# Batch 0's second half: keys mixed two rows at a time, queries turned by full transposes, and a warm-up of 64 short and 5 wide matmuls

## The chip, the cores and the metric

The kernel runs on one core of one Trainium2 chip, in one launch. The metric is the device time of one execution in microseconds. A core has TensorE (matmuls and the loads of their weights, listed in the profile as PE and PEld), VectorE (DVE), ScalarE (ACT), GpSimd (POOL) and SyncE (SP). Each engine works off its own instructions in order and waits for others by semaphores; transfers go through DMA queues that SP and POOL feed here. Matmuls write to PSUM, and VectorE or ScalarE must copy a result out before its PSUM buffer can be used again.

## What is computed

Two layers follow each other. The first is a block-sorted attention: a small 8x8 matrix per head is normalized five times over rows and columns (Sinkhorn) and then mixes the eight blocks of keys and of values; each block of 96 queries attends only to its own mixed block. The second is a mixture of four experts over the attention's output.

```python
def _attn_ref(q, k, v, sort_net):            # q, k, v: (4, 8, 768, 64); sort_net: (4, 8, 8, 8)
    P = sort_net
    for _ in range(5):
        P = P - np.max(P, axis=-1, keepdims=True)
        P = np.exp(P)
        P = P / (np.sum(P, axis=-1, keepdims=True) + 1e-09)
        P = P / (np.sum(P, axis=-2, keepdims=True) + 1e-09)
    k_sorted = np.einsum('bhij,bhjcd->bhicd', P, k_b)      # k_b: k in 8 blocks of 96 rows
    v_sorted = np.einsum('bhij,bhjcd->bhicd', P, v_b)
    scores = scale * np.matmul(q_b, k_sb.transpose(0, 1, 2, 4, 3))
    attn = softmax(scores)
    return np.matmul(attn, v_sb)

def _moe_ref(x, domain_probs, w1, w2):       # x: (3072, 512); w1: (4, 512, 1024); w2: (4, 1024, 512)
    p = domain_probs / (domain_probs.sum(-1, keepdims=True) + 1e-09)
    for e in range(E):
        h = np.maximum(x @ w1[e], 0.0)
        out += p[:, e:e + 1] * (h @ w2[e])
```

## The kernel before

The order of the instructions on every engine is the order in which the kernel's text issues them; nothing reorders them. The work is staged by batch. Batches 1 to 3 go by plans of small steps slotted between the experts' matmuls. Batch 0 has its own code, because everything waits for it at the start; the change lies there, in the first 33 us.

Start: one DVE memset makes a constant tile `dummy`, and `warm(84)` issues 84 matmuls of 128x128 on it (L260) whose results nobody reads, while ScalarE and VectorE go through the five normalizations (L295 to L315). Within the fifth, the queries of the first half are transposed (`h_q`, L272) and 30 more such matmuls follow. When the normalized weights are there, they are spread by four matmuls (L327) and multiplied with a mask into `PI0`, a 128x64 matrix per head and half: a product with it mixes the blocks.

Batch 0's data lie in "natural" layout: partition p holds six consecutive rows (R = 6) of each head, so that sixteen partitions (CP = 16) are one block. The eight heads form two quads (`qd` 0, 1), the eight output blocks two halves (`hf` 0, 1) of four (HB = 4). `mix_half` makes one quad's half: for each head and each row r it multiplies a 128x64 slice of the keys (or values) as weights with the 64 columns of `PI0` (L506), 24 matmuls. Two heads write to partitions 0 to 63 and 64 to 127 of the same PSUM buffer, each on one half of TensorE's columns. `mixed` copies the buffer out (L517) with one copy of 128x768 when it takes a whole half. `h_k` does both for the keys, into `kTs[qd]`, the operand of the scores; `h_v` for the values, into `vT0[qd]`. `h_w` (L533) transposes mixed values back, `h_s` (L561) computes scores and their exponentials (L567), `h_a` (L578) multiplies with the values and normalizes (L591, L592), `h_x` (L609) transposes the result into `xTs[0]`, the input of the experts, and copies it out (L613).

Between these, the first layer of expert 0 runs in groups: `group0(qq, nq, g, kcs)` (L690) accumulates over the four chunks `kcs` of the 512 inputs and, after the last, ScalarE applies relu and writes `Hb` (L703). `second_layer0` (L725) multiplies with the second weights; after its first four matmuls of each output tile, and after each tile, it calls the next entry of the list `later`. The first entry is `h_q_both(1, vec)` and `h_w(1, vec)`: the 48 transposes of 64x64 for the queries of the second half, both quads, with two VectorE copies (L285), and a transpose of values.

Queries of batch 0 are loaded to `q0` (in the room of `Tt[3]`) by POOL's DMAs of line L147: quad 0 on partitions 0 to 63, quad 1 on 64 to 127. The second half's are issued at 12.6 and 13.3 us.

PSUM buffers come from two pools of two: `psm` (TensorE's results of the experts, and others) and `psa` (the attention's). A pool gives out a buffer again only when the last reader of what stood there is through; the matmul that writes to it first waits for that.

Of the kernel before, what the change touches and what calls it, by code (L numbers as in the profile page):

```python
# [9 lines left out]
F32 = mybir.dt.float32  # L10
F16 = mybir.dt.float16
# [6 lines left out]
def kernel(  # L18
# [11 lines left out]
    nc = tc.nc  # L30

    B, H, S, D = q.shape
# [6 lines left out]
    P = 128  # L39
    SCALE = float(D) ** -0.5  # L40

    CP = P // NB
    R = BLK // CP
# [3 lines left out]
    HB = NB // 2  # L47
# [75 lines left out]
    def head(b, nm, h):  # L123
        return natural[(b, nm, h // 4)][:, h % 4, :, :]
# [26 lines left out]
    dummy = Hflat[:, ds(2 * NFC * 2 * P, P)]  # L151
# [16 lines left out]
    ident = const.tile([P, P], F16, name="ident")  # L168
# [84 lines left out]
    qTs = {}  # L253
    q_ring = const.tile([P, 3, R, P], F16, name="q_ring")

    def warm(n):
        ps = psM.tile([P, 4, P], F32, tag="ps", name=f"ps_w_{state['n']}")
        state["n"] += 1
        for m in range(n):
            nc.tensor.matmul(ps[:, m % 4, :], dummy, dummy, start=True, stop=True)  # L260

    qT0 = [from_spare(2 * S).rearrange("p (s f r x) -> p s f r x", s=2, f=2, r=R) for _ in range(2)]

    def h_q(qd, hf, copy, ps=None):

        if ps is None:
            ps = psa([P, 2, R, 64], F16, f"ps_q_{qd}_{hf}")
        rows = ds(64 * qd, 64)
        for sg in range(2):
            for r in range(R):  # L270
                for hh in range(2):
                    nc.tensor.transpose(  # L272
                        ps[ds(D * hh, D), sg, r, :], q0[rows, hf, 2 * sg + hh, r, :], ident[rows, rows]
                    )
        if copy:
            copy(qT0[qd][:, :, hf], ps[:])

    def h_q_both(hf, copy):

        ps = psa([P, 2, 1024], F16, f"ps_q_{hf}")  # L280
        pss = [ps[:, qd, 0:2 * R * 64].rearrange("p (s r x) -> p s r x", s=2, r=R) for qd in range(2)]
        for qd in range(2):
            h_q(qd, hf, None, pss[qd])
        for qd in range(2):
            copy(qT0[qd][:, :, hf], pss[qd])  # L285
# [210 lines left out]
    def mix_half(nm, qd, hf, pool, warm_up=0):  # L496

        ps = pool([P, 1024], F32, f"ps_m{nm}_{qd}_{hf}")
        keep_warm(ps[:, 0:P], warm_up)
        tails[(nm, qd, hf)] = ps[:, 2 * R * 64:1024].bitcast(F16).rearrange("p (n x) -> p n x", n=2)  # L500
        ps = ps[:, 0:2 * R * 64].rearrange("p (s r x) -> p s r x", s=2, r=R)
        for sg in range(2):
            for r in range(R):
                for hh in range(2):
                    h = 4 * qd + 2 * sg + hh
                    nc.tensor.matmul(  # L506
                        ps[ds(D * hh, D), sg, r, :],
                        head(0, nm, h)[:, r, :],
                        PI0[hf][:, h, :, :].rearrange("p i c -> p (i c)"),
                        start=True, stop=True,  # L510
                    )
        return ps

    def mixed(nm, qd, ps, i0, n, copy):

        dst = kTs[qd][:, 0:S] if nm == "k" else vT0[qd]
        copy(  # L517
            dst.rearrange("p (i x c) -> p x i c", i=HB, c=CP)[:, :, ds(i0, n)],
            ps.rearrange("p s r (i c) -> p (s r) i c", c=CP)[:, :, ds(i0, n)],
        )  # L520
# [80 lines left out]
    def h_x(qq, copy, qds=range(2), ps=None, warm_up=0):  # L601

        nq = len(qds)
        if ps is None:
            ps = psa([P, 2, 512], F32, f"ps_x0_{qq}_{qds[0]}")
        keep_warm(ps[:, 0, 0:P], warm_up)
        for m, qd in enumerate(qds):
            for n in range(4):
                nc.tensor.matmul(  # L609
                    ps[:, m, ds(n * BLK, BLK)], xsl0[(qd, qq)][:, n, :, :].rearrange("c h d -> c (h d)"),  # L610
                    perm[:], start=True, stop=True,
                )
        copy(  # L613
            xTs[0][:, :, ds(2 * qq, 2), :].rearrange("p (q s) i x -> p q s (i x)", q=2)[:, ds(qds[0], nq)],
            ps[:, 0:nq, 0:4 * BLK].rearrange("p q (s x) -> p q s x", s=2),
        )
# [60 lines left out]
    def group0(qq, nq, g, kcs=range(NKC), later=False):  # L677

        n = nq * HS // 2
        m = KH // nq
        xT = xTs[0].rearrange("p k i x -> p k (i x)")
        if (qq, g) not in groups:
            open_group(qq, g)
        ps = groups[(qq, g)]
        whole = len(kcs) == NKC
        for f in range(m):
            for kc in kcs:
                nc.tensor.matmul(  # L690
                    ps[:, f % 2 if nq == 2 else f // 2, ds(0 if nq == 2 else (f % 2) * n, n)],
                    w1sb[0][:, kc, ds((m * g + f) * P, P)],
                    xT[:, kc, ds(qq * HS // 2, n)],
                    start=(kc == 0 and (whole or f % 2 == 0)),
                    stop=(kc == NKC - 1 and (whole or f % 2 == 1)),
                )
        if kcs[-1] < NKC - 1:
            return
        at = (0, 3)[m * g // KH] * NFC * 2 * P + (m * g % KH) * HS
        h = Hflat[:, ds(at, m * HS)]  # L700

        def evacuate():
            nc.scalar.activation(  # L703
                h.rearrange("p (a x) -> p a x", a=2) if nq == 2
                else h.rearrange("p (a f x) -> p a f x", a=2, f=2)[:, :, :, ds((qq % 2) * n, n)],
                ps[:, :, 0:n] if nq == 2 else ps[:, :, 0:2 * n].rearrange("p a (f x) -> p a f x", f=2),
                AF.Relu, bias=0.0, scale=1.0,
            )

        if later:  # L710
            return evacuate
        evacuate()
# [718 lines left out]


    load_w1(1)
# [7 lines left out]
    def builds(b):  # L1441
# [47 lines left out]
    for g in range(G0 + 1):  # L1489
        b, c = divmod(g, R // 2)  # L1490
# [56 lines left out]
```

## Time and profile before

| what | us |
| --- | --- |
| three runs | 358.77, 358.48, 358.75 |
| median | 358.75 |
| the profiled execution | 358.5 |
| its span, first to last instruction | 356.7 |
| TensorE busy in the span | 350.4 |
| VectorE busy | 277.2 |
| ScalarE busy | 169.2 |
| stretch 23 to 32 us: PE, DVE, ACT busy | 9.00, 6.38, 3.77 of 9 |

A line of the timeline has the start of a merged run of equal instructions, its length, the engine, the line of the kernel, the operation, what it writes and reads, shapes, and a count; in brackets stands the engine's idle time before it and who ended it. A matmul's length goes from its start to the end of its result and overlaps the next one's, so the difference of two starts is what a group takes of TensorE. TensorE's granted clock is 1.00 throughout. The profiled time is 1.8 us longer than the span: that is the work around the first and the last instruction.

### The profile page before, as it was taken

Reading aid. Unit: us, or ns where it says so; the run is one execution under the profiler, and the core shown is the slowest. Engines: PE = TensorE matmul, PEld = TensorE weight load, DVE = VectorE, ACT = ScalarE, POOL = GpSimd, SP = SyncE. Lnnn points to the kernel's source line nnn. Section 1 sums busy time; section 2 is a strip of 40 time slices with the busy share of each in tenths; the row PEclk is TensorE's granted clock in tenths of the full one; section 3 lists DMA queues with packets and bytes.
Section 4 is the critical chain, followed back from the end, with each engine's and each line's share of the span. In section 5 each row is a group of like instructions: output and inputs, shape, how many; then the busy total and the mean of one; then the engine's idle time right before and its main releaser. Section 6 shows DMA issues by size and latency. Waiting matters only on the chain.

```text
span 356.7 us, 9498 instructions
## 1 busy us (share of the span) xinstructions
PE 350.4 (98%) x3949; PEld 305.6 (86%) x3949; DVE 277.2 (78%) x553; ACT 169.2 (47%) x302; POOL 133.5 (37%) x149
## 2 busy tenths in 40 slices
PE   8799999999999999999999999999999999999996
PEld 8686857888888888888899888888888888888885
DVE  5757797779798687778889978896588876588963
ACT  2653330452425445368937158830388511688201
POOL 8873010466022330000535318840068800288400
PEclk9999999999999999999999999999999999999999
DMA  8999999999999999844994310005200015100011
GB/s 116 208 206 229 214 210 198 205 190 178 185 189 163 184 130 198 141 88 68 170 212 69 114 66 0 2 2 136 85 17 2 3 47 131 62 0 2 2 74 46
DMA packets 72022, 40.51 MB, mean 114 GB/s; under 512 B 40614, under 2 KB 66732, under 8 KB 71980
## 3 DMA queue, kind: packets, MB, share of 16 engines
q0 software_dynamic: 36576, 19.93, 42.2%
q1 hardware_dynamic: 35260, 19.92, 28.3%
q8 instruction: 31, 0.51, 0.6%
q14 instruction: 11, 0.09, 0.1%
q10 hardware_dynamic: 144, 0.07, 0.1%
HBM read 42.13 MB, written 6.34 MB: 136 GB/s over the span
## 4 chain that ended last, share of the span: by engine, by line
PE 94%; DVE 2%; POOL 2%; DMA 0%; issue 0%; ACT 0%
PE ps_h L801 18%; PE ps_Q L1275 18%; PE ps_p L785 12%; PE ps_X L1132 10%; PE ps_Z L1132 7%; PE ps_Q L1132 7%; PE ps_Z L1275 6%; PE ps_o L725 3%; PE ps_h L690 3%; PE ps_p L841 3%; PE ps_a L464 2%; PE ps_s L429 2%; PE ps_k L410 1%; PE ps_v L376 1%; PE ps_a L578 0%; POOL sn L315 0%
## 5 line engine op out<-in xcount | busy, mean ns | idle before, releaser
L801 PE MATMUL ps_h<-xT,w 128*128 128x256 f16 x576 | 67.5, 273 | 0.0
L801 PEld LDWEIGHTS <-w 128*128 128x128 f16 x576 | 55.2, 98 | 7.3
L807 DVE SCALAR_TENSOR_TENSOR Hb<-ps_h,pb 128x1024 f16<-128x1024 f32 x34 | 41.5, 1223 | 17.8 <-PE ps_h L801 17.2
L1132 PEld LDWEIGHTS <-w 128*128 128x128 f16 x480 | 43.6, 98 | 4.7
L1145 POOL TENSOR_TENSOR arena<-tmp,pb 128x512 f16<-128x512 f32 x12 | 15.2, 1276 | 65.7 <-PE ps_Z L1132 49.8
L1275 PEld LDWEIGHTS <-Hb 128*128 128x128 f16 x320 | 31.1, 98 | 3.5
L1144 ACT ACTIVATE tmp<-tmp 128x512 f32<-128x512 f32 x46 | 29.0, 632 | 3.9 <-DVE tmp L1182 3.9
L1275 PEld LDWEIGHTS <-Sb 128*128 128x128 f16 x304 | 28.2, 98 | 3.0
L1132 PEld LDWEIGHTS <-arena 128*128 128x128 f16 x312 | 27.7, 98 | 2.9
L436 ACT ACTIVATE ET<-ps_s 96x768 f16<-96x768 f32 x24 | 18.0, 802 | 25.1 <-PE ps_s L429 24.8
L419 ACT CAST kT<-ps_k 64x384 f16<-64x384 f32 x48 | 22.7, 473 | 13.3 <-PE ps_k L410 12.3
L121 POOL DMA_DIRECT2D arena<-in_q_dram x24 | 19.9, 844 | 17.7 <-DMA q_ring<-arena 17.7
L1132 PE MATMUL ps_X<-ET,arena 128*128 128x256 f16 x168 | 25.2, 272 | 0.0
L1275 PE MATMUL ps_Q<-w,Hb 128*128 128x256 f16 x192 | 24.6, 273 | 0.0
L785 PEld LDWEIGHTS <-Hb 128*128 128x128 f16 x232 | 21.8, 98 | 3.0
L1138 DVE SCALAR_TENSOR_TENSOR Hb<-ps_X,pb 128x512 f16<-128x512 f32 x27 | 18.7, 691 | 7.0 <-PE ps_X L1132 7.0
L1152 ACT COPY ps_X<-ps_Z 128x512 f32<-128x512 f32 x27 | 15.4, 571 | 17.8 <-PE ps_Z L1132 17.8
L1132 PE MATMUL ps_Z<-xT,w 128*128 128x256 f16 (+1 forms) x176 | 22.5, 258 | 0.0
L771 DVE TENSOR_TENSOR Sb<-Hb 128x512 f16<-128x512 f16 x33 | 20.5, 646 | 0.0
L1159 ACT COPY tmp<-ps_X 128x512 f32<-128x512 f32 x26 | 15.2, 585 | 9.2 <-PE ps_X L1132 6.6
L1138 DVE SCALAR_TENSOR_TENSOR Hb<-ps_Z,pb 128x512 f16<-128x512 f32 x27 | 18.4, 682 | 1.3 <-PE ps_Z L1132 1.3
L1182 DVE TENSOR_TENSOR tmp<-ps_Q,tmp 128x512 f32<-128x512 f32 x26 | 17.7, 682 | 0.8 <-PE ps_Q L1132 0.8
(266 smaller groups left out, 739.4 us busy)
## 6 DMA issues: line engine op xcount, KB each, us to landing
w<-in_moe_w_dram POOLq DMA_DIRECT2D x6, 1024.0 KB, 28.4
pb<-p_dram SPq DMA_DIRECT2D x9, 512.0 KB, 7.3
arena<-in_k_dram POOLq DMA_DIRECT2D x8, 384.0 KB, 8.9
arena<-in_v_dram POOLq DMA_DIRECT2D x8, 384.0 KB, 7.9
vs<-arena SPq DMA_DIRECT2D x36, 66.0 KB, 5.6
arena<-in_q_dram POOLq DMA_DIRECT2D x24, 96.0 KB, 8.3
out_dram<-ob SPq DMA_DIRECT2D x9, 256.0 KB, 2.0
w<-in_moe_w_dram POOLq DMA_DIRECT2D x4, 512.0 KB, 12.4
```

Source lines behind the costliest of these rows:

```text
L121: nc.gpsimd.dma_start(t[:, h // 2, :, h % 2, :], q[b, h].rearrange("(t p) d -> p t d", p=P))
L419: nc.scalar.copy(kT[ds(D * hh, D), r], pk[ds(D * r, D), hh].rearrange("p a (i c) -> p a i c", c=CP),)
L436: nc.scalar.activation(ETs[2 * (pr % 2) + hh][:, 0:S].rearrange("c (a x) -> c a x", a=2), pss[hh][0:BLK, :, 0:HS], AF.Exp, bias=0.0, scale ...
L771: tt(sm[0], blk(0, 1), blk(1, 1), ALU.add)
L785: nc.tensor.matmul(ps, lhs(e, f), Ts[e][rhs][:, f, :], start=(first and e == es[0] and f == 0), stop=(done and e == es[-1] and f == KH - 1 ...
L801: nc.tensor.matmul(ps[:, f, :], w1sb[e][:, kc, ds((4 * g + f) * P, P)], xT[:, kc, ds(2 * c * P, 2 * P)], start=(kc == 0), stop=(kc == NKC ...
L807: nc.vector.scalar_tensor_tensor(out=Hb[:, homes.get(e, e), ds(4 * g, 4), :], in0=ps[:], scalar=0.0, op0=ALU.max, in1=weights(e).broadcast ...
L1132: nc.tensor.matmul(dst[:, ds(f * cols, cols)], a[lhs][:, k, ds((f0 + f) * P, P)], t[rhs][:, k, :], start=(first and f == 0 and k == 0), st ...
L1138: nc.vector.scalar_tensor_tensor(out=home(i, j), in0=src.rearrange("p (f x) -> p f x", f=m), scalar=0.0, op0=ALU.max, in1=weight(j).broadc ...
L1144: nc.scalar.activation(src, src, AF.Relu, bias=0.0, scale=1.0)
L1182: tt(t12, Q, u2, ALU.add)
L1275: nc.tensor.matmul(ps, lhs(e, f), Ts[e][rhs][:, f, part], start=(first and e == 0 and f == 0), stop=(e == E - 1 and f == KH - 1), skip_gro ...
```

## The change

Four things, all in batch 0's opening:

- `warm` gets a width. `warm(84)` becomes `warm(64)` and `warm(5, 4)`: five matmuls with a moving operand of 4 x 128 columns, the same tile read four times.
- The second half's keys (`h_k(qd, 1)`) go through the new `half_k`: two rows r of a head at a time as a full 128x128 weight tile, 12 matmuls a quad in place of 24. The two rows come out on partitions 0 to 63 and 64 to 127, so four copies of 64x384 (`hh`, `r`) bring them to `kTs` in place of one of 128x768: on ScalarE for quad 0, on VectorE for quad 1.
- The second half's queries are first put side by side by ScalarE (`pair_q(sg)`: a copy of 128x768 in SBUF, from `q0` to `q1`, which lies in the still free `Tt[1]`), both quads on 128 partitions. Then `half_q` does 12 transposes of 128x128 in place of 48 of 64x64, and two VectorE copies as before.
- The order changes: `group0(1, 1, 1)` opens its first chunk ahead of `h_x(1, vec, [1])` and takes the second behind it, and `h_v(0, 1)` and `h_v(1, 1)` stand behind the group's last two chunks rather than ahead of them.

No DMA is added, removed or moved; SP's and POOL's instructions keep their order.

```diff
-    def warm(n):
+    def warm(n, wide=1):
         ps = psM.tile([P, 4, P], F32, tag="ps", name=f"ps_w_{state['n']}")
         state["n"] += 1
         for m in range(n):
-            nc.tensor.matmul(ps[:, m % 4, :], dummy, dummy, start=True, stop=True)
+            nc.tensor.matmul(
+                ps[:, ds(m * wide % 4, wide), :],
+                dummy, dummy.rearrange("p (o x) -> p o x", o=1).broadcast_to([P, wide, P]), start=True, stop=True,
+            )
...
-    def h_q_both(hf, copy):
-
-        ps = psa([P, 2, 1024], F16, f"ps_q_{hf}")
-        pss = [ps[:, qd, 0:2 * R * 64].rearrange("p (s r x) -> p s r x", s=2, r=R) for qd in range(2)]
-        for qd in range(2):
-            h_q(qd, hf, None, pss[qd])
-        for qd in range(2):
-            copy(qT0[qd][:, :, hf], pss[qd])
...
-    warm(84)
+    warm(64)
+    warm(5, 4)
...
+    def half_k(qd, copy):
+
+        ps = psa([P, 2, 512], F32, f"ps_k0_{qd}")
+        pk = ps[:, :, 0:R * 64].rearrange("p h (x i c) -> p h x i c", x=R, c=CP)
+        for hh in range(2):
+            for sg in range(2):
+                h = 4 * qd + 2 * sg + hh
+                for a in range(R // 2):
+                    nc.tensor.matmul(
+                        ps[:, hh, ds((sg * (R // 2) + a) * 64, 64)],
+                        head(0, "k", h)[:, ds(2 * a, 2), :].rearrange("p r d -> p (r d)"),
+                        PI0[1][:, h, :, :].rearrange("p i c -> p (i c)"),
+                        start=True, stop=True,
+                    )
+        kT = kTs[qd][:, 0:S].rearrange("p (i x r c) -> p r x i c", i=HB, r=2, c=CP)
+        for hh in range(2):
+            for r in range(2):
+                copy(kT[ds(D * hh, D), r], pk[ds(D * r, D), hh])
+
+    q1 = Tt[1].rearrange("p a f x -> p (a f x)")[:, 0:2 * R * P].rearrange("p (s r x) -> p s r x", s=2, r=R)
+
+    def pair_q(sg):
+
+        nc.scalar.copy(
+            q1[:, sg].rearrange("p r (h d) -> p r h d", h=2),
+            q0[:, 1, ds(2 * sg, 2)].rearrange("p h r d -> p r h d"),
+        )
+
+    def half_q(copy):
+
+        ps = psa([P, 2, 1024], F16, "ps_q1")
+        for sg in range(2):
+            for r in range(R):
+                nc.tensor.transpose(ps[:, sg, ds(r * P, P)], q1[:, sg, r], ident[:])
+        for qd in range(2):
+            copy(
+                qT0[qd][:, :, 1],
+                ps[:, :, 0:R * P].rearrange("p s (r q x) -> p s r q x", r=R, q=2)[:, :, :, qd],
+            )
...
     group0(0, 1, 1, [2, 3])
     h_a(1, 1, ps_s11)
-    h_k(0, 1, act)
+    pair_q(0)
+    half_k(0, act)
     group0(1, 1, 0, [0, 1])
+    group0(1, 1, 1, [0])
     h_x(1, vec, [1], ps_s11)
-    group0(1, 1, 1, [0, 1])
-    h_k(1, 1, vec)
+    group0(1, 1, 1, [1])
+    half_k(1, vec)
     group0(1, 1, 0, [2, 3])
+    pair_q(1)
+    group0(1, 1, 1, [2, 3])
     h_v(0, 1, vec)
     h_v(1, 1, vec)
-    group0(1, 1, 1, [2, 3])
...
     later = [
-        [(h_q_both, 1, vec), (h_w, 1, vec)],
+        [(half_q, vec), (h_w, 1, vec)],
```

More of the change, by code (lines that the diff above doesn't have):

```diff
@@ L259, in warm, with h_q @@
         for m in range(n):
-            nc.tensor.matmul(ps[:, m % 4, :], dummy, dummy, start=True, stop=True)
+            nc.tensor.matmul(
+                ps[:, ds(m * wide % 4, wide), :],
+                dummy, dummy.rearrange("p (o x) -> p o x", o=1).broadcast_to([P, wide, P]), start=True, stop=True,
+            )
     qT0 = [from_spare(2 * S).rearrange("p (s f r x) -> p s f r x", s=2, f=2, r=R) for _ in range(2)]
-    def h_q(qd, hf, copy, ps=None):
-        if ps is None:
-            ps = psa([P, 2, R, 64], F16, f"ps_q_{qd}_{hf}")
+    def h_q(qd, hf, copy):
+        ps = psa([P, 2, R, 64], F16, f"ps_q_{qd}_{hf}")
         rows = ds(64 * qd, 64)
@@ L274, in h_q @@
                     )
-        if copy:
-            copy(qT0[qd][:, :, hf], ps[:])
-    def h_q_both(hf, copy):
-        ps = psa([P, 2, 1024], F16, f"ps_q_{hf}")
-        pss = [ps[:, qd, 0:2 * R * 64].rearrange("p (s r x) -> p s r x", s=2, r=R) for qd in range(2)]
-        for qd in range(2):
-            h_q(qd, hf, None, pss[qd])
-        for qd in range(2):
-            copy(qT0[qd][:, :, hf], pss[qd])
+        copy(qT0[qd][:, :, hf], ps[:])
     srow = const.tile([GH, NB, 1], F32, name="srow")
```

## The prediction, made before the changed kernel was run

> **What bounds the kernel now.** I read the page's busy shares first, then TensorE's waits over the whole span, then the timeline of the stretch that the change touches.
>
> ```profile
> PE 350.4 (98%) x3949; PEld 305.6 (86%) x3949; DVE 277.2 (78%) x553; ACT 169.2 (47%) x302; POOL 133.5 (37%) x149
> ```
>
> ```profile
> PE ps_R L327 <- DVE sn L315: 1.4, 1, 1.4
> PE ps_w L260 <- DVE Hb L152: 1.1, 1, 1.1
> ```
>
> The second view lists everything that TensorE waited for visibly: 1.1 us for its first operand, 1.4 us (10.39 to 11.80) for the normalized weights. After 12 us it has no wait of that size. So a microsecond of TensorE time saved or lost after 12 us goes to the end undiminished; one before 11.8 us goes into the 1.4 us hole. The timeline of the changed stretch (start, length, engine, line):
>
> ```profile
> 22.63 1.52 ACT L703 ACTIVATE Hb<-ps_h 128x768 f16<-128x768 f32 x2
> 22.72 0.41 PE L578 MATMUL ps_a<-Sb,ET 96*128 96x65 f16 x8
> 23.05 0.57 PE L506 MATMUL ps_mk<-Sb,arena 128*64 128x64 f16 x24
> 23.55 0.83 PE L690 MATMUL ps_h<-xT,w 128*128 128x192 f16 x8
> 24.22 0.34 PE L609 MATMUL ps_a<-perm,xsl 96*128 96x96 f16 x4
> 24.40 0.82 PE L690 MATMUL ps_h<-xT,w 128*128 128x192 f16 x8
> 24.60 0.56 DVE L613 CAST xT<-ps_a 128x384 f16<-128x384 f32 x1 [0.45 <-PE ps_a L609]
> 25.15 0.57 PE L506 MATMUL ps_mk<-Sb,arena 128*64 128x64 f16 x24
> 25.65 0.83 PE L690 MATMUL ps_h<-xT,w 128*128 128x192 f16 x8
> 26.42 0.95 PE L506 MATMUL ps_mv<-Sb,arena 128*64 128x64 f16 x48
> 27.03 1.82 DVE L517 CAST Sb<-ps_mv 128x768 f16<-128x768 f32 x2 [0.31 <-PE ps_mv L506]
> 27.30 0.83 PE L690 MATMUL ps_h<-xT,w 128*128 128x192 f16 x8
> 27.97 1.03 PE L725 MATMUL ps_o<-w,Hb 128*128 128x512 f16 x4
> 28.92 0.85 PE L272 MATMUL ps_q<-ident,T 64*64 64x64 f16 x48
> 29.70 0.65 PE L533 MATMUL ps_w<-ident,Sb 128*96 128x128 f16 x8
> 29.81 1.02 DVE L285 COPY Sb<-ps_q 128x768 f16<-128x768 f16 x2 [0.97 <-PE ps_q L272]
> ```
>
> Differences of PE starts are what each group occupies; there are no holes. The last two views are 128-column weights with short moving operands, and copies of 64 partitions:
>
> ```profile
> 35.15 0.40 PE L578 MATMUL ps_a<-Sb,ET 96*128 96x65 f16 x8
> 35.39 1.03 PE L725 MATMUL ps_o<-w,Hb 128*128 128x512 f16 x4
> ```
>
> ```profile
> 67.73 1.96 ACT L419 CAST kT<-ps_k 64x384 f16<-64x384 f32 x4 [0.85 <-PE ps_k L410]
> ```
>
> **What TensorE saves.** Going into and out of matmuls on a part of the array costs time beside their own. The eight 65-column matmuls take 0.24 us at 35.15 (30 ns each) but 0.33 us at 22.72, ahead of the half-width mix; eight L690 matmuls take 0.67 us at 23.55 but 0.75 us at 24.40. So the two key mixes cost 0.09 + 0.50 = 0.59 and 0.08 + 0.50 = 0.58 us. The 48 query transposes: four L725 matmuls take 0.95 us at 27.97 against 4 x 0.216 = 0.86 us (24 of them take 5.18 us at 50.45), so 0.09, plus 0.78, plus 0.04 for the slow first L533 behind them: 0.91 us. Removed: 2.08 us. Added: twice 12 matmuls of 128x128 weights and 64 columns, at the 30 ns of the 65-column row: 0.36 us each (bounds: 29 ns as measured there, 56 ns if it goes like the 128-column L533 row, whose eight take 0.45 us); and 12 full transposes at 56 ns: 0.67 us. Added: 1.39. Saved: 0.69 us, were nothing waited for.
>
> The Trainium skill speaks against the last price: "TensorE: Matmul & The Clock Gate", section "Back-to-back issue gap", gives about 81 ns for each weight load and matmul of 128 columns in a real kernel. By that the 12 transposes are 0.97 us, 0.30 us more, and the change ends 0.30 us later than below; this trace's 56 ns decide.
>
> **The waits that come in.** The order of the built program shows four waits on TensorE that the shorter work runs into. I walk through them in times of this profile; from an engine's end to the waiting matmul I take 0.06 us (L592 ends at 19.94, L609 starts at 20.00), from a last matmul's end to a copy 0.04 us (24.56 to 24.60).
>
> 1. half_k(0) runs from 22.72 + 0.24 = 22.96 to 23.32. Group (1,1,0) needs the bank that the first L703 empties: 22.63 + 0.81 + 0.06 = 23.50. Its first eight matmuls end at 24.16. Group (1,1,1), now opened earlier, waits for the second L703: 24.15 + 0.06 = 24.21; its key-chunk 0 ends at 24.54, h_x at 24.71, chunk 1 at 25.04. Of the first mix's gain 0.22 us are gone already.
> 2. half_k(1) now takes the PSUM buffer that h_x's copy on VectorE must empty (before, the second mix waited for ScalarE's copy of the first, at 24.84). h_x's result is there at 24.54 + 0.34, copied from 24.92 to 25.48, so half_k(1) starts at 25.54: a hole of 0.50 us with everything queued behind it. It ends at 25.90; its result is complete at 25.54 + 11 x 0.030 + 0.20 = 26.07.
> 3. The two remaining group parts end at 26.56 and 27.22; h_v(0) starts 0.09 later, at 27.31. Its buffer needs ScalarE's four copies of half_k(0): ScalarE is free of L703 at 24.03, pair_q(0) takes it until 24.73 (priced as the 0.77 us L276 copy of the same 128x768, less overlap; up to 1.05 by the 1024-element SBUF copy L1008), then 1.96 us as L419: 26.69. That is 0.6 us (0.3 us at the other bound) before it is needed: hidden. pair_q(0)'s data landed at 22.6 us, as POOL's wait for it until 22.90 shows; later than 24.1 us it would hold the copies and then the evacuations behind it. pair_q(1) and the last L703 end near 29.0, ahead of the transposes that read it (29.8) and the second output tile.
> 4. h_v(1), ready at 27.31 + 0.38 = 27.69, needs the buffer of half_k(1), now emptied by four VectorE copies of 64x384 in place of one of 128x768 (0.96 us). The trace has no such copy on VectorE. A 128x384 one lasts 0.56 us (L613). If they overlap as L517's two do (1.82 us for 2 x 0.95) one starts every 0.475 us; if they don't, as L419's don't on ScalarE (1.96 us for four of 0.473: every 0.497 us, longer than they last), every 0.58 us. I take 0.58: L419 is this very pattern, halves of partitions alternating. The four run from 26.11 to 26.11 + 3 x 0.58 + 0.56 = 28.41, so h_v(1) starts at 28.47: a hole of 0.78 us (0.46 us at 0.475). Behind it stand the second layer, half_q and all the rest.
>
> The skill has a rule for VectorE itself: "VectorE: DVE Perf Modes", section "Two Vector instructions with no wait between them", holds an instruction until the earlier ones have finished when its start quadrant differs from what was last read or written. The copies alternate partitions 0 and 64, so by it they do not overlap and the sum is the +0.9 us below, against +0.58 us without it; no VectorE row of this trace shows it.
>
> From there: h_v(1) 0.50 us with its way out (48 such matmuls take 0.88, 24 of them 0.38), to 28.97; four L725 to 29.83; half_q's buffer waits for h_v(0)'s copy (28.43 + 0.96 + 0.06 = 29.45, in time); 12 transposes to 30.50. Before, h_w stood at an effective 29.74: 0.76 us late. Last, VectorE copies the queries only when all 12 transposes are through, 0.20 us after h_w's start against 0.07 before, and the scores of the second quad wait for h_w's copy behind that (before, it ended at 31.43 and they started at 31.49): 0.13 us more. **Sum: +0.9 us** (+0.58 with overlapping copies; +1.2 with 56 ns matmuls in half_k(1)).
>
> **The warm-up.** 20 short matmuls at 56 ns become 5 wide ones at 0.216 us: 1.12 against 1.08 us, ending near 7.7 us as before. The next stage starts at 11.80 by VectorE's result, so this counts nothing; even five at twice the length end some 0.3 us before the hole does. Without that cover it would be a gain of 0.04 us.
>
> **The number.** Span 356.7 and 1.8 us around it are the profiled 358.5 us; the median of three runs, 358.75, is 0.25 above. 358.75 + 0.9 = 359.65. For this kernel 0.2% is 0.72 us, about what a measurement can tell from no change.
>
> **Rivals.** *Copies overlap* on VectorE (0.475 us apart): +0.58, 359.3, within 0.2%. For it: L517's and L285's pairs overlap. Against: L419. *VectorE never binds* (the not-slower side): if a 64-partition copy cost half of a 128-partition one, 0.28 us, four would be done by 27.23 and h_v(1) would not wait; the line is 27.69 - 0.06 - 26.11 = 1.52 us, 0.38 us a copy. Then the sum is +0.9 - 0.78 = +0.12, 358.9. If half_k(1) also found a free buffer, 0.4 to 0.5 us less: 358.4. Against it: L419's 0.473 us on 64 partitions equals L613's 0.478 us on ScalarE for 128, so half the partitions save nothing, and the built order names the wait. Even the whole 0.69 us falls short of 0.72: faster by over 0.2% needs something not in these steps. *Short matmuls at 56 ns*: +1.2, 359.95.
>
> **Chances.** Forecast 0.68 (its own 359.4 to 359.9; a little of it, 0.08, lies under 0.72), overlap 0.10, VectorE never binding 0.06, slow matmuls 0.06, something unlisted that makes it faster 0.10. Slower 0.60 + 0.06 = 0.66, same 0.08 + 0.10 + 0.06 = 0.24, faster 0.10. The range 358.85 to 360.1 leaves out the last case and the tail beyond slow matmuls.
>
> **What would show it.** Right: TensorE waits for h_x's VectorE copy ahead of half_k(1) (0.5 us) and for half_k(1)'s copies ahead of h_v(1) (0.8 us), the copies some 0.58 us apart, half-width mixes gone with their ways in and out, everything after 33 us shifted by one constant near 0.9. Wrong: no PE wait between 24 and 29 us, copies under 0.4 us, or a shift that first shows before 12 us or after 33 us.

## The result, and the profile after

| | median us | from | to | ratio to before, 95% interval |
| --- | --- | --- | --- | --- |
| before, the runs beside it | 358.66 | 358.48 | 359.22 | |
| the changed kernel | 360.94 | 359.91 | 362.52 | 1.0053 [1.0031, 1.0076] |

The change costs 2.3 us by these medians. The direction is the one predicted; the time lies 1.3 us above the forecast and 0.84 us above the range. The profiled execution took 362.52 us, the longest of the six, so it shows more lost time than the others had; the five others have no profile.

First TensorE's busy share and its waits over the span (engine and line that waits, what it waited for, us in total, times, longest):

```profile
PE 351.4 (97%) x3874; PEld 305.5 (85%) x3874; DVE 278.2 (77%) x556; ACT 171.7 (48%) x307; POOL 133.6 (37%) x149
```

```profile
PE ps_h L723 <- DMA w<-in_moe_w_dram: 1.4, 1, 1.4
PE ps_h L834 <- DVE Hb L840: 1.3, 1, 1.3
PE ps_w L260 <- DVE Hb L152: 1.1, 1, 1.1
PE ps_R L320 <- DVE sn L308: 0.9, 1, 0.9
PE ps_mv L499 <- DVE kT L535: 0.6, 1, 0.6
PE ps_k L526 <- DVE xT L646: 0.3, 1, 0.3
```

Before, this list had only the two waits ahead of 12 us. The last two are those of the prediction: h_v(1) (L499) waits for half_k(1)'s copies, half_k(1) (L526) for h_x's copy. The first two were not in it. L723 waits at 21.3 us for the second half of the first expert's first weights; L834, at 99 us, for VectorE, and VectorE in turn for `pb`, the experts' shares:

```profile
99.17 2.36 DVE L840 SCALAR_TENSOR_TENSOR Hb<-ps_h,pb 128x1024 f16<-128x1024 f32 x2 [2.85 <-PE ps_k L403]
```

The profile puts this wait down to TensorE's L403, whose semaphore came last before it. L840 does not read what L403 writes; it reads `pb`, which landed at 99.08 us, 0.09 us ahead of its start. In e2, e6 and e10 (shown below) the profile names `pb` for the same wait.

The changed stretch in the timeline (the columns as before):

```profile
22.66 0.83 PE L723 MATMUL ps_h<-xT,w 128*128 128x192 f16 x8 [1.39 <-DMA w<-in_moe_w_dram]
...
24.16 0.41 PE L611 MATMUL ps_a<-Sb,ET 96*128 96x65 f16 x8
...
24.41 0.51 PE L526 MATMUL ps_k<-Sb,arena 128*128 128x64 f16 x12
...
24.95 1.19 PE L723 MATMUL ps_h<-xT,w 128*128 128x192 f16 x12
...
25.98 0.34 PE L642 MATMUL ps_a<-perm,xsl 96*128 96x96 f16 x4
...
26.96 0.51 PE L526 MATMUL ps_k<-Sb,arena 128*128 128x64 f16 x12 [0.32 <-DVE xT L646]
...
27.31 1.48 PE L723 MATMUL ps_h<-xT,w 128*128 128x192 f16 x16
27.51 2.31 DVE L535 CAST kT<-ps_k 64x384 f16<-64x384 f32 x4 [0.60 <-PE ps_k L526]
...
28.72 0.57 PE L499 MATMUL ps_mv<-Sb,arena 128*64 128x64 f16 x24
...
29.88 0.57 PE L499 MATMUL ps_mv<-Sb,arena 128*64 128x64 f16 x24 [0.59 <-DVE kT L535]
...
30.38 1.04 PE L758 MATMUL ps_o<-w,Hb 128*128 128x512 f16 x4
...
31.25 0.83 PE L551 MATMUL ps_q<-ident,T 128*128 128x128 f16 x12
...
31.92 0.61 PE L566 MATMUL ps_w<-ident,Sb 128*96 128x128 f16 x8
```

The stretch starts 1.44 us late (L611 at 24.16 against 22.72), mostly by the wait for the weights. Less that shift, the predicted walk and the trace stand side by side:

| step | predicted start | measured, less 1.44 |
| --- | --- | --- |
| h_x (L642) | 24.54 | 24.54 |
| half_k(1) (L526) | 25.54 | 25.52 |
| its first copy (L535) | 26.11 | 26.07 |
| h_v(0) | 27.31 | 27.28 |
| h_v(1) | 28.47 | 28.44 |
| second layer (L758) | 28.97 | 28.94 |
| half_q (L551) | 29.83 | 29.81 |
| h_w (L566) | 30.50 | 30.48 |

So the walk holds to 0.04 us. To see where the rest came from, I laid the TensorE instructions of the two traces side by side, counted back from the last one, and took the difference of their starts, each from its own span's start. I call it the lateness; the times at which I give it are those of the kernel before. In this profile it is 2.30 us at 33 us (0.91 without the 1.39 us hole at 21 us), goes to 3.73 at 97 us, to 4.03 at 160 us, and is 4.02 at the end. The profiled execution is accounted for by it: 358.50 + 4.02 = 362.52 us.

### The profile page after: what moved, and what is told of

Read it like the earlier page. It is cut to its first block, busy times and chain, and to the rows that moved or that the text cites. A ratio compares the mean times of both kernels' runs of the same rounds, so it can differ in the third digit from the quotient of the medians.

```text
span 360.8 us, 9358 instructions
## 1 busy us (share of the span) xinstructions
PE 351.4 (97%) x3874; PEld 305.5 (85%) x3874; DVE 278.2 (77%) x556; ACT 171.7 (48%) x307; POOL 133.6 (37%) x149
## 4 chain that ended last, share of the span: by engine, by line
PE 89%; DMA 5%; POOL 1%; DVE 1%; SPq 1%; issue 1%; ACT 1%; ACTq 0%; POOLq 0%
PE ps_Q L1308 17%; PE ps_h L834 16%; PE ps_p L818 12%; PE ps_X L1165 10%; PE ps_Z L1165 7%; PE ps_Q L1165 7%; PE ps_Z L1308 6%; DMA w<-in_moe_w_dram 4%; PE ps_o L758 3%; PE ps_p L874 3%; PE ps_h L723 2%; PE ps_a L457 2%; PE ps_s L422 1%; PE ps_k L403 1%; SPq L383 1%; PE ps_v L369 1%
## 5 line engine op out<-in xcount | busy, mean ns | idle before, releaser
L834 PE MATMUL ps_h<-xT,w 128*128 128x256 f16 x576 | 67.5, 273 | 1.3 <-DVE Hb L840 1.3
L834 PEld LDWEIGHTS <-w 128*128 128x128 f16 x576 | 55.2, 98 | 8.7 <-issue 1.4
L840 DVE SCALAR_TENSOR_TENSOR Hb<-ps_h,pb 128x1024 f16<-128x1024 f32 x34 | 41.4, 1223 | 19.6 <-PE ps_h L834 16.6
L804 DVE TENSOR_TENSOR Sb<-Hb 128x512 f16<-128x512 f16 x33 | 20.6, 647 | 0.0
```

The source lines that it names most:

```text
L804: tt(sm[0], blk(0, 1), blk(1, 1), ALU.add)
L834: nc.tensor.matmul(ps[:, f, :], w1sb[e][:, kc, ds((4 * g + f) * P, P)], xT[:, kc, ds(2 * c * P, 2 * P)], start=(kc == 0), stop=(kc == NKC ...
L840: nc.vector.scalar_tensor_tensor(out=Hb[:, homes.get(e, e), ds(4 * g, 4), :], in0=ps[:], scalar=0.0, op0=ALU.max, in1=weights(e).broadcast ...
```

## The experiments

All ran in alternation with the kernel before; "fastest" is the shortest execution. "Key path" is the lateness at 33 us less the hole that a weight transfer made ahead of it; "later" is what the profile adds from 33 us to the last TensorE instruction.

| run | fastest | median | ratio, 95% interval | key path | later |
| --- | --- | --- | --- | --- | --- |
| before (in all comparisons) | 358.48 | 358.66-359.11 | | 0 | 0 |
| changed, first | 359.91 | 360.94 | 1.0053 [1.0031, 1.0076] | 0.91 | 1.72 |
| e5 changed, second | 359.62 | 359.91 | 1.0036 [1.0022, 1.0051] | 0.99 | 0.36 |
| e13 changed, third | 359.70 | 360.54 | 1.0044 [1.0028, 1.0059] | 0.96 | 0.23 |
| e1 warm-up alone | 358.60 | 359.00 | 0.9995 [0.9986, 1.0003] | 0.09 | 0 |
| e2 keys and queries | 359.57 | 359.94 | 1.0026 [1.0015, 1.0036] | 0.92 | 1.04 |
| e3 keys alone | 360.19 | 360.63 | 1.0042 [1.0027, 1.0058] | 1.54 | 0 |
| e6 queries alone | 358.70 | 358.96 | 1.0010 [0.9995, 1.0025] | -0.12 | 1.69 |
| e4 before + 16 matmuls | 359.72 | 361.06 | 1.0049 [1.0031, 1.0067] | 1.23 | 0 |
| e7 copies alternate | 360.49 | 360.81 | 1.0062 [1.0045, 1.0079] | 1.39 | 0.59 |
| e9 one copy | 358.99 | 359.51 | 1.0008 [0.9995, 1.0022] | 0.14 | 0.64 |
| e8 pb moved | 359.44 | 360.08 | 1.0031 [1.0018, 1.0043] | 0.91 | 0.38 |
| e10 pb and vs moved | 359.46 | 359.56 | 1.0015 [1.0003, 1.0028] | 0.87 | 0.66 |
| e14 the same again | 359.44 | 359.84 | 1.0020 [1.0010, 1.0030] | 0.92 | 0.10 |
| e11 changed, loads early | 359.35 | 359.58 | 1.0027 [1.0007, 1.0048] | 0.82 | 2.56 |
| e12 before, loads early | 358.52 | 359.22 | 0.9997 [0.9983, 1.0011] | 1.05 | 0.10 |
| e15 changed, code moved | 359.86 | 360.75 | 1.0040 [1.0023, 1.0056] | 0.94 | 0.43 |
| e16 before, code moved | 358.52 | 360.15 | 1.0027 [1.0009, 1.0044] | 0.07 | 0 |
| e17 before, code further | 358.71 | 359.40 | 1.0018 [1.0005, 1.0030] | -0.01 | 0.75 |

**The parts of the change.** e1 is the kernel before with the new warm-up; e2 the changed kernel with the old one; e3 the kernel before with the new keys and order; e6 with the new queries.

```diff
@@ e1, the kernel before @@
-    warm(84)
+    warm(64)
+    warm(5, 4)
@@ e2, the changed kernel @@
-    warm(64)
-    warm(5, 4)
+    warm(84)
@@ e3, the kernel before, with the change's order of groups and values @@
-    h_k(0, 1, act)
+    half_k(0, act)
...
-    h_k(1, 1, vec)
+    half_k(1, vec)
@@ e6, the kernel before @@
     h_k(0, 1, act)
+    pair_q(0)
...
     group0(1, 1, 0, [2, 3])
+    pair_q(1)
...
-        [(h_q_both, 1, vec), (h_w, 1, vec)],
+        [(half_q, vec), (h_w, 1, vec)],
```

> Before, with the new warm-up alone (64 short and 5 wide matmuls). Theory A (the key path's waits cost 0.85 us, and being late costs more at the transfers between 75 and 100 us): no change, within 0.3 us of before, no hole at 21 us. Theory B (the warm-up delays the first transfers, so that the second half of the first expert's weights lands too late): 0.4 to 1.5 us slower than before, with TensorE waiting for that transfer near 21 us.

> The changed kernel with the old warm-up of 84 short matmuls. Theory A: as the changed kernel, 1.3 to 2.5 us slower than before. Theory B: 0.9 us slower than before, TensorE's wait at 21 us gone.

> Only the keys in pairs of rows, with the change's order of the groups; the old warm-up and the old 64x64 query transposes. By the steps of the prediction 0.24 us of the transposes' saving is given back and 0.13 us of the later copies too: holes ahead of half_k(1) and h_v(1) of 0.3 to 0.8 us each remain, about 1.0 us late at 33 us. Theory A: 1.2 to 2.5 us slower in all, with a hole near 99 us. Theory B: 1.0 us slower, nothing later.

> The kernel before with the new path of the queries alone (pair copies on ScalarE, 12 full transposes, half-and-half copies), keys and warm-up as before. By the prediction's steps: 48 transposes with their ways in and out 0.91 us go, 12 at 56 ns come (0.67): -0.24, and +0.13 for the later VectorE copies: -0.1 us, ratio 0.9997, nothing measurable. Rival (any change of the stretch between 22 and 32 us costs, since the transposes' copies or pair_q stand in ScalarE's way): +0.5 us or more, ratio over 1.0015, with a TensorE hole between 24 and 33 us.

The warm-up alone does not change the time measurably (ratio 0.9995), although its profile has a hole of 0.8 us at 21 us, which Theory A had excluded. e2, with the old warm-up, has no such hole, and its median is 0.8 us above before's, as Theory B had it; but its path is as late (0.92 us), e1 is no slower, and the hole also comes with the old warm-up (e3, 0.4 us). So the warm-up is not what makes the change late. The queries alone gain 0.12 us on the path and nothing measurable in the time, and the lateness is the keys'. e3 lost more than expected, 1.54 us on the path, by a longer first wait:

```profile
PE ps_k L536 <- ACT kT L545: 0.8, 1, 0.8
PE ps_mv L509 <- DVE kT L545: 0.6, 1, 0.6
```

In e3 half_k(1) waited for all four of ScalarE's copies of half_k(0) instead of h_x's one on VectorE: the pool gave it the other of its two buffers. So a part taken alone need not wait as it does in the whole; why the buffers fall otherwise here was not followed.

**Lateness alone.** e4 is the kernel before with 16 needless matmuls of 128x128 ahead of a group.

```diff
     h_a(1, 1, ps_s11)
     h_k(0, 1, act)
+    open_group(1, 1, 16)
     group0(1, 1, 0, [0, 1])
```

> Before, with 16 more dummy matmuls of 128x128 (0.9 us of TensorE time at 56 ns) ahead of the first layer's last group at 24 us, and nothing else changed. Theory A: more than those 0.9 us, 1.3 to 2.3 us slower, because being late brings the hole near 99 us. Theory B, and a third, C (what comes after 33 us differs from run to run whatever the kernel): 0.9 us slower, a shift that stays constant to the end in most runs.

Its fastest execution, the profiled one, is 1.22 us over before's fastest beside it (358.50), as its lateness of 1.23 us says. The 16 matmuls are 0.89 of it; the other 0.34 us appear at 30 us, with a pause of TensorE of 0.16 us for which the profile names no releaser. The lateness then stays constant to the end, so in this execution a delay did go to the end as it was. The median is 1.95 us over the 359.11 beside it: its executions spread over 2.6 us (1.6 us without the slowest, whose granted clock was 0.991), with the old keys and queries.

**The second wait.** e9 makes half_k(1)'s four copies one, of the shape the kernel had before, which leaves the keys of heads 4 to 7 in the wrong places; e7 tried to hide both waits while keeping every result.

```diff
@@ e9, the changed kernel, in half_k @@
+        if qd:
+            copy(kTs[qd][:, 0:S].rearrange("p (h x) -> p h x", h=2), ps[:, :, 0:R * 64])
+            return
@@ e7, the changed kernel, an engine for each (hh, r) @@
-                copy(kT[ds(D * hh, D), r], pk[ds(D * r, D), hh])
+                copy[2 * hh + r](kT[ds(D * hh, D), r], pk[ds(D * r, D), hh])
...
-    half_k(0, act)
+    half_k(0, (vec, act, act, act))
...
-    half_k(1, vec)
-    group0(1, 1, 0, [2, 3])
+    group0(1, 1, 0, [2])
+    half_k(1, (vec, act, vec, act))
+    group0(1, 1, 0, [3])
```

> The changed kernel with half_k(1)'s four VectorE copies of 64x384 replaced by one of 128x768 from the same PSUM tile; the keys of heads 4 to 7 in the second half of batch 0 then stand in the wrong places. Theory (h_v(1)'s hole is the four copies, started one after the other 0.58 us apart): one copy of 0.96 us ends 1.4 us earlier, the 0.59 us hole ahead of h_v(1) goes, the 0.32 us ahead of half_k(1) stays, the lateness at 33 us falls from 0.92-0.99 to 0.3-0.45, and the time from 359.9 to 359.0-359.4 (the lower end if the hole at 161 us closes too). Rival (h_v(1) is held by something else, such as h_v(0)'s copy or the group's evacuation behind it): the hole stays above 0.3 us, time as the changed kernel's.

> The changed kernel with the two waits of half_k(1) and h_v(1) given cover and nothing else: the first of half_k(0)'s four copies goes to VectorE, half_k(1)'s are shared two and two between VectorE and ScalarE, and one key-chunk of group (1,1,0) runs ahead of half_k(1). Theory (these two waits are the lateness): both holes vanish, half_k(1)'s last copy ends 1.1 us earlier, the lateness at 33 us is -0.1 to +0.1 us apart from what the hole at 21 us brings, and the time is that of the kernel before: 358.4 to 359.2, ratio 0.999 to 1.001. Rival (the waits are replaced by others, ScalarE's evacuations of the groups now stand behind more copies): a new hole ahead of the second layer or of h_v, ratio 1.002 or more.

In e9's timeline the copy takes 0.96 us, and the two h_v run without a hole, as one group of 48:

```profile
26.43 0.96 DVE L533 CAST kT<-ps_k 128x768 f16<-128x768 f32 x1 [0.60 <-PE ps_k L526]
...
27.64 0.95 PE L499 MATMUL ps_mv<-Sb,arena 128*64 128x64 f16 x48
```

The path falls from 0.91 to 0.14 us, further than expected, and the fastest execution by 0.63 us (359.62 in e5 to 358.99). So the four copies are the main price of the change. e7 was a miss. Its timeline of the two copying engines:

```profile
26.38 0.55 DVE L535 CAST kT<-ps_k 64x384 f16<-64x384 f32 x1 [0.93 <-PE ps_k L526]
...
27.02 0.47 ACT L535 CAST kT<-ps_k 64x384 f16<-64x384 f32 x1 [0.71 <-DVE kT L535]
...
27.53 0.55 DVE L535 CAST kT<-ps_k 64x384 f16<-64x384 f32 x1 [0.60 <-ACT kT L535]
...
28.11 0.47 ACT L535 CAST kT<-ps_k 64x384 f16<-64x384 f32 x1 [0.62 <-DVE kT L535]
```

Each copy waits for the other engine's: the program orders them by semaphores, presumably because they share a PSUM tile and interleaved columns of one destination; the reason was not tested. Shared, they end 2.20 us after the first start, against 2.31 us on VectorE alone, and the hole ahead of h_v(1) grew to 0.8 us. The group's chunk put ahead of half_k(1) waited for h_x's copy just as half_k(1) had (0.32 us, L723 <- DVE xT), since chunks 2 and 3 are what that copy writes.

**The two late places.** e8 issues the third load of `pb` on ScalarE's queue, e10 and e14 also three of the six `vs` copies near 155 us. e11 and e12 take the changed kernel and the one before, add this, and leave out a load of 384 KB ahead of the first weights, the values of heads 4 to 7 (those of heads 0 to 3 stand in for them). In the expectations w1(0) is the first expert's first weights.

```diff
@@ e8, the load of pb @@
-        nc.sync.dma_start(
+        (nc.scalar if (b, c) == (0, 2) else nc.sync).dma_start(
@@ e10 and e14, besides: the copies of vs @@
-                nc.sync.dma_start(
+                (nc.scalar if (b, qd) == (3, 0) and r % 2 else nc.sync).dma_start(
@@ e11 and e12, besides: load_natural @@
+        if (b, nm, qd) == (0, "v", 1):
+            natural[(b, nm, qd)] = natural[(0, "v", 0)]
+            return
```

> The changed kernel as it is, beside the others of this call. Theory (the key path's waits make it 0.9 us late, and work that is late by a microsecond loses a further 0.3 to 2 us at two transfers whose landing varies, the second half of w1(0) near 21 us and pb near 99 us): ratio again 1.003 to 1.007, about 360.5, and the profile shows holes of 0.3 us ahead of half_k(1) and 0.6 us ahead of h_v(1) as in the first profile, while the holes at 21 and 99 us differ in size from the 1.39 and 1.27 us there. Rival (the lateness beyond 0.9 us belongs to the change itself): the holes at 21 and 99 us come back at the same size, lateness at the end about 4 us.

> The changed kernel with one transfer moved: the load of pb for the third chunk is issued on ScalarE's queue in place of SP's, where it stands behind two transposing loads of queries and six copies of vs. Theory (the 1.27 us hole at 99 us is SP's queue running late: the load was issued at 88.6 us and landed at 99.1, though its buffer was free at 85.0): issued near 85 us, landed before 96 us, no hole at 99 us, the lateness from 33 us on stays constant up to 150 us; the time comes down by the mean of that hole over the executions, 0.3 to 1 us, and its spread narrows. Rival (the DMA engines are full and the load lands late whatever its queue): landing at 97 us or later, same time as the changed kernel.

> The changed kernel with its arithmetic and order untouched and two transfers taken off SP's queue: the load of pb for the third chunk, and three of the six copies of vs that run near 154-160 us, both issued on ScalarE's queue. Theory (beyond the 0.95 us of the key path, the loss is made at these two places by SP's queue): no hole at 97-99 us and none at 161 us, the lateness is constant from 33 us to the end at 0.9 to 1.0 us when the hole at 21 us is absent, and the time is 359.4 to 359.7. Rival (other transfers bind next, or ScalarE's issue time delays its copies): the lateness still grows by 0.3 us or more after 33 us.

> The changed kernel as in the run before, and in addition the values of heads 4 to 7 of batch 0 are not loaded (those of heads 0 to 3 are used in their place), so that w1(0) is transferred 384 KB earlier. Theory (the second half of w1(0), needed at 21.3 us and landing between 20.1 and 22.6, is the variable part of the early loss): it lands 1.5 to 2 us earlier, before 21 us in every execution, the hole at 21 us is gone, and the run differs from the next one (the kernel before with the same) by the key path alone: 0.8 to 1.0 us, ratio of the two 1.0022 to 1.0028. Rival (the change costs more than its two waits even with these transfers out of the way): a difference of 1.3 us or more.

> The kernel before with the same three alterations: pb for the third chunk and half of the vs copies near 154 us on ScalarE's queue, and the values of heads 4 to 7 of batch 0 not loaded. Theory: it has no hole of its own at 21, 97 or 161 us in most executions, so it gains little in the median (358.3 to 358.8) and loses its slow tail. Rival (the kernel before also loses at these transfers in most executions): under 358.2.

> The changed kernel a third time. Theory (a fixed 0.9 us from the key path, 0.2 us at 161 us, and a variable loss at transfers): its fastest executions stand at 359.6 to 359.7, its median anywhere from 359.8 to 361, ratio 1.003 to 1.005; the two holes at half_k(1) and h_v(1) are 0.3 and 0.6 us again. Rival (the first comparison's 1.0053 is the change's own cost): no execution under 359.9, median 360.7 or more.

> The changed kernel with pb's third load and three vs copies on ScalarE's queue, a second time and beside the changed kernel itself. Theory: fastest executions 359.45 to 359.5, 0.1 to 0.2 us under the changed kernel's, half of the executions within 0.15 us of the fastest, and no hole at 161 us. Rival (the transfers bind wherever they are issued from): same fastest time and the same spread as the changed kernel.

In e5 and e13 neither the hole at 21 us nor that near 97 us came back. So their size is not the change's own, as the theory of e5 had it; the median of e5, 359.91 us, was lower than the 360.5 expected.

Near 97 us VectorE waited for `pb` in the kernel before too. Its own timeline has this line, without a TensorE hole behind it; the same view of e10 stands below:

```profile
94.43 1.22 DVE L807 SCALAR_TENSOR_TENSOR Hb<-ps_h,pb 128x1024 f16<-128x1024 f32 x1 [0.40 <-DMA pb<-p_dram]
```

```profile
96.87 2.35 DVE L840 SCALAR_TENSOR_TENSOR Hb<-ps_h,pb 128x1024 f16<-128x1024 f32 x2 [1.97 <-DMA pb<-p_dram]
```

In e10 `pb` was issued at 83.6 us, 5 us sooner than in the first profile, and yet it landed at 96.8 us with a hole of 0.4 us; in e8 it was issued at 83.7 and landed at 94.1, without one; in e5 and e13, untouched, it was issued near 86.2 and landed at 94.5 and 93.6. So the landing is not set by SP's queue alone, as I had held: 7.6 to 13.2 us pass between issue and landing, and that differs between executions. e6, without the keys, had the largest of these holes (1.48 us). The lateness gives the time of need: in the four profiles with such a hole (the first, e2, e6 and e10) it rises there by 1.44, 0.50, 1.65 and 0.56 us, and the landing less this rise and less the lateness ahead of it is 95.3 us each time. By this, an estimate, `pb` came 1.0 us ahead of TensorE's need in the profile of before (94.34 us).

The hole at 21 us is of the same sort. TensorE needs the second half of the weights at 21.2 us. It landed at 20.1 us in the profile of before, at 22.0 in e1 and e16, at 22.6 in the first of the changed kernel, between 20.6 and 21.6 in the others, kernels with and without the new keys mixed. e6 waited for the first half instead, 0.68 us until 19.8. In e11 and e12 the second half landed at 19.2 and 19.3, and neither has that hole. Their fastest executions differ by 0.83 us, those of e10 and of before beside it (358.50) by 0.96: with the transfers in time, in these executions, the change costs what its steps say. The medians show it less clearly: four of e11's twelve executions took 361.39 us or more, and its profile, one of them, waited 0.9 and 1.0 us for transfers between 193 and 199 us. e12's median, 359.22 us, is above what was expected (358.3 to 358.8): its slow tail did not go. Its profile holds two pauses of TensorE, of 0.7 and 0.3 us, for which it names no releaser (1.05 us in the table).

Moving `vs` has a price of its own: in e10, e11, e12 and e14 ScalarE spends 2.2 us on issuing the three copies, its next exponentials start later, and TensorE loses 0.10 us near 156 us in each. e14's fastest execution, 359.44 us, is 0.26 us under that of the changed kernel beside it, but only four of its eleven executions lie within 0.15 us of it, not half.

**A loss that came with the program's length.** Apart from e3, every run so far with the new keys lost another 0.2 to 0.6 us at 160 us, unless `vs` was moved (e10, e14, e11); before, e1, e3, e4 and e6 did not. SP's timeline of before, then of e5, over the six copies:

```profile
153.12 3.79 SPq L390 DMA_DIRECT2D vs<-arena  x6
```

```profile
154.10 4.55 SPq L383 DMA_DIRECT2D vs<-arena  x6
```

One issue of the six took 1.37 us in place of 0.6, the last copy landed at 160.63 us, ScalarE waited for it, and TensorE's scores for ScalarE's PSUM copy. In the list of DMA packets one of 16 KB on the instruction queue starts at 156.68 us, the slow issue at 156.65. The seven profiles with this loss have an issue of 1.2 to 1.6 us in this set, and in each such a packet starts within 0.3 us of it; in before, e1, e3 and e4 none falls among the copies (before: 150.7 and 161.0). e6 lies between: its packet starts at 155.09 us, 0.2 us ahead of the first copy, one issue took 0.98 us, and nothing was lost. The change takes 75 matmuls out of TensorE's program, and the packets on this queue shift; that they load TensorE's program is inferred from this. Three runs moved them by the warm-up alone, trading short matmuls for wide ones with the same total of 10752 columns.

```diff
@@ e15, the changed kernel @@
-    warm(64)
-    warm(5, 4)
+    warm(4)
+    warm(20, 4)
@@ e16, the kernel before @@
-    warm(84)
+    warm(24)
+    warm(15, 4)
@@ e17, the kernel before @@
-    warm(84)
+    warm(21, 4)
```

> The changed kernel with warm(64), warm(5, 4) replaced by warm(4), warm(20, 4): the same 10752 columns, 45 matmuls (90 instructions with their weight loads) fewer. At some 18 instructions per us of that stretch the instruction packets come 4 to 5 us later: from 156 to about 161 us, and the one before from 146 to 151. Theory (the packet that falls on the vs copies holds up SP's issue and costs the 0.2 to 0.6 us near 161): all six issues take 0.6 us, no hole at 161 us, fastest executions 359.4 to 359.5. Rival (the coincidence is chance; the copies are slow because the DMA engines are busy): a vs issue of 1.2 us or more at 154 to 159 us remains and the fastest executions stay at 359.6 or above.

> The kernel before with warm(84) replaced by warm(24), warm(15, 4): the same 10752 columns, 45 matmuls fewer, nothing else. Theory: the packet that came at 150.7 us comes near 155.5 us, in the middle of the six vs copies (153.1 to 156.9 us): one of them takes 1.2 us or more, ScalarE's next copy waits for it, TensorE is 0.2 to 0.5 us later from 161 us on, and the fastest executions stand at 358.7 to 359.0 in place of 358.5. Rival (the packet is not the cause): fastest executions at 358.5 and no slow vs issue there.

> The kernel before with warm(84) replaced by warm(21, 4): the same 10752 columns, 63 matmuls fewer, nothing else. Ninety instructions fewer moved the packet from 150.7 to 153.6 us (of which 0.9 is the lateness of that profile); 126 fewer should bring it to 154.5-155.5 us, among the vs copies. Theory (the packet holds up SP's issue): one of the six issues at 153 to 158 us takes 1.2 us or more and the packet starts within 0.2 us of it. Rival (chance): all six take 0.6 us although a packet falls among them.

e15's packet went to 160.7 us, and SP's timeline is that of before again:

```profile
154.38 3.78 SPq L383 DMA_DIRECT2D vs<-arena  x6
```

But the next one now met the following set: it starts at 171.66 us, the issue at 171.8 took 1.74 us, and a TensorE hole of 0.3 us came at 179.5 (L457 <- DMA vs). The loss had moved, and the time did not improve. In e16 the packet fell at 153.6, just ahead of the copies, and did nothing. In e17 it hit. The DMA queues of e17 between 154 and 155 us (packets, MB, share of 16 engines), SP's six copies, ScalarE's next copy, and TensorE's wait for it:

```profile
q1 hardware_dynamic: 139, 0.07, 26.0%
q8 instruction: 1, 0.02, 9.1%
```

```profile
153.10 4.94 SPq L393 DMA_DIRECT2D vs<-arena  x6
...
160.24 0.80 ACT L385 CAST arena<-ps_v 128x768 f16<-128x768 f32 x1 [1.62 <-DMA vs<-arena]
```

```profile
PE ps_s L432 <- ACT arena L385: 0.6, 1, 0.6
```

The packet starts at 154.27 us, the issue at 154.37 took 1.75 us, and a kernel whose lateness was -0.01 us at 33 us is 0.74 us late at the end: its profiled execution took 359.25 us, before's 358.50. Nothing but the warm-up differs, and its results nobody reads. With e15, where the packet left these copies and the loss at 160 us went, this shows the cause of the loss. It does not show what the packet does inside SP or the DMA engines; a slow issue also comes without one, since the last issue of the next set, near 172 us, takes 1.1 to 1.5 us in 18 of the 19 profiles. Nor is the loss the same in every execution: e17's fastest took 358.71 us, 0.18 over the fastest of before beside it.

## Why the prediction came out as it did

**Right: the walk through 22 to 33 us.** TensorE's saving, both waits and their order held to 0.04 us, and the sum of 0.9 us stands against 0.82 to 0.99 us in the nine profiles that have the whole of keys and queries unaltered (e2, e5, e8, e10, e11, e13, e14, e15 and the first).

- Key matmuls at 30 ns: 0.36 us predicted; half_k(1) takes 0.35 (26.96 to 27.31). The rival of 56 ns falls.
- Transposes at 56 ns, 0.67 us: measured 0.67 (31.25 to 31.92), and 0.67 in e6. The Trainium skill's 81 ns ("TensorE: Matmul & The Clock Gate", "Back-to-back issue gap") would have been 0.97.
- Copies 0.58 us apart: four took 2.31 us, 0.585 apart. The rival of overlapping copies falls: each starts 0.03 us after the end of the one before it, and the last three wait for no semaphore. What the Trainium skill says in "VectorE: DVE Perf Modes", "Two Vector instructions with no wait between them", agrees with it: an instruction that starts in another quadrant is held until the earlier one is through.
- VectorE never binding falls with e9: without the four copies the same path is 0.14 us, with them 0.91.
- The hole ahead of half_k(1), given as 0.50, is 0.48 by the starts (26.15 + 0.33 to 26.96); the listed 0.32 counts from the modelled end of the last matmul.

**Wrong: the step from the path to the time.** The prediction read from two waits ahead of 12 us that a microsecond lost after 12 us "goes to the end undiminished", and added 0.9 us to the median as the whole effect. The 0.9 us do arrive at the end, but the step put every later wait, and every late transfer, at nothing without a term for it. A shift that first shows after 33 us was among its own signs of being wrong, and in the first profile 1.72 of 4.02 us came after 33 us, and 1.39 in the hole at 21 us ahead of the changed stretch. Two kinds of loss came on top of the path.

One is the 0.2 to 0.6 us near 160 us, in all seven profiles where a packet fell among SP's copies with the new keys. The paragraph on the warm-up says that "this counts nothing" because its time is covered, and no step asks what a program 75 matmuls shorter does elsewhere. e17 shows that hidden matmuls can cost 0.75 us by where the packets on the instruction queue fall. With it the profiled executions without a late weight or `pb` are accounted for: from the 358.50 of before's profile, 0.99 + 0.36 make 359.85 for e5, whose profiled execution took 359.85, and 0.96 + 0.23 make 359.69 for e13, which took 359.70.

The other is larger where it occurs, and varies: transfers that land close to their need, near 21 us (0 to 1.4 us) and near 97 us (0 to 1.5 us). Both showed in the trace of before, the second as VectorE's 0.40 us wait for `pb` (1.0 us ahead of TensorE's need, by the estimate above), the first as a landing at 20.14 us for a need at 21.2; the prediction looked only at TensorE's waits, where a transfer that is just in time leaves no line. These losses also meet kernels without the new keys (e1, e6, e16), so they do not need the change.

What stays open is the size of the varying part, and with it the median that was to be predicted: only one execution of each comparison has a profile, so where the execution at the median lost its time is inferred. The changed kernel's median was 360.94, 359.91 and 360.54 us in three comparisons, each beside 358.66 to 359.10 for before; the first, with which the forecast was compared, was the highest, and 8 of the 22 executions took 360.1 us or less. A lower granted clock is not the reason: one of the 22 shows less than 0.998 (0.995, at 361.79 us). As to the kernels before, e4 and e16, which have neither new keys nor new queries, reached 361.06 and 360.15 with fastest executions of 359.72 and 358.52. Whether a late kernel meets these transfers more often, or whether it is chance of the executions, was not separated.

No version was measurably faster than the kernel before. The queries alone shorten the path by 0.12 us, which the times cannot show (ratio 1.0010 [0.9995, 1.0025]).

## What to carry to other kernels

Halving a matmul's count by filling the array can move its cost to whoever empties PSUM: here 12 fewer matmuls a quad came with four copies in place of one, and a copy did not get cheaper with half the partitions. When a shift is carried to the end of a long kernel, list every transfer with less margin than the shift plus its own spread, on all engines, and not only the waits that TensorE shows. A measured difference of a few tenths of a microsecond between two programs of different length may be where the packets on the instruction queue fall: move them with harmless instructions before believing a cause.

## What the runs showed of the hardware

A packet of 16 KB on the instruction queue comes every 5 to 20 us here, and the SP issues of `vs` copies that it met near 155 and 172 us took 1.0 to 1.75 us instead of 0.6 (0.98 in e6, 1.24 in e13, 1.37 in e5, 1.75 in e17). Copies of 64x384 last about as long as of 128x384 on VectorE (0.55 and 0.56 us). The same 512 KB load of `pb` took 7.6 to 13.2 us from issue to landing in different executions of nearly the same program.
